# Small softmax turned by a transposing transfer, small steps spread over the engines, squares without a bias

## The chip, the cores and the metric

The kernel runs on one core of one Trainium2 chip. The metric is the device time of one execution in microseconds; of the kernel before three executions are known, and one more was taken with a profile. The core has TensorE (matrix products into PSUM), VectorE, ScalarE and GpSimd, which run side by side, each through its own list of instructions in order. SyncE (SP) issues all transfers here, also in order. In the profile the engines are PE, PEld (TensorE's weight loads), DVE, ACT, POOL and SPq.

## The reference

Four batches of 12608 tokens with 128 channels are computed in two parts. First agent attention with 49 agents a batch, and then a feed-forward layer of width 1024 whose activation is h times softmax(h), followed by a layer norm:

```python
a2k = sm(agents, k)            # softmax of the scaled products over 12608 keys
agent_v = a2k @ v              # 49 x 128 for each batch
q2a = sm(q, agents)            # "small softmax": 49 logits for each token
x = (q2a @ agent_v).reshape(B * S, 128)

h = x @ w_in                   # 128 -> 1024
e = np.exp(h - h.max(-1))
solu = h * e / (e.sum(-1) + 1e-9)
ln = (solu - mean(solu)) / sqrt(var(solu) + 1e-6) * g_ln
out = ln @ w_out               # 1024 -> 128
```

The factors 1/sqrt(128) and 1e-9 of the softmaxes are in the kernel; q, k and the agents are drawn eight times larger than unit inputs times 0.1.

## The kernel before

**Tiles.** A tile `x` is 128 tokens; there are 394, in four batches of 98 or 99. Two half tiles that are left at the ends of two batches share one tile (`both`). Units of 8 tiles (`UB`, 52 in all) go through the small softmax together.

**Phase A, once a batch** (`phase_a`). Keys and values come in 13 chunks of 512 KB each. For each chunk there are products with the agents (line 601), the chunk's maximum (`p1_max`, 606), the running maximum (`p1_nm`, line 613, VectorE), the exponential (627), four transposes, an eviction, and products with the values. At the end `agent_v` is multiplied into `w_in`, which gives 49 x 1024 matrices in two f16 halves. For batches 1 to 3 this is spread over the tiles of the batch before.

**Phase B, once a unit** (`phase_b`). Queries are loaded, logits made (863), maximum (869), subtraction (875), exponential (879), sum and reciprocal (883, 886). The result is packed as two f16 parts, high by ScalarE or GpSimd (`b4h`) and low by GpSimd (`b4l`, 897), into `packs`. Then TensorE turns the tiles four at a time into a PSUM bank (`b5`, line 904), and ScalarE or VectorE evicts the four to a buffer `pT` (`b6`, line 910), one of five (`PTB`).

**Steps of a tile.** H: four matmuls of `pT` with the matrices into one of two `ph` (955). Maximum and scaling on VectorE (983). Exponential on ScalarE (990). `u` = h times e on VectorE (998), with the sum of u accumulated into a cell `su`. The square on ScalarE (1019), with `su` as bias, sums the squared distances from the mean for the layer norm. Then u must be turned for the last product. For 331 tiles (`xbar`) GpSimd or ScalarE makes an f16 high half (`c_f0`, 1004 or 1006), GpSimd the low half (`c_f1`, 1009), and one transposing transfer of 128 x 2048 f16 on SP (`c_x`, line 1013) turns both into a buffer of the ring `xr` of eight (`XB`); 24 matmuls follow (1047). For the other 63 TensorE turns u in f32 (1026), ScalarE or VectorE evicts (1031) into a ring `tr` of eight (`TBUF`), and 16 passes follow. For each group of 8 or 16 tiles (27 groups) `c_rstd` makes the factor of the layer norm from the sums in a chain of short steps on GpSimd and ScalarE (1062 to 1085). VectorE multiplies four tiles of the product by it out of PSUM (`c_fin`, 1092), and a transfer writes eight tiles out (1098).

**Order.** The Python code makes a list of 6999 operations, each with the engines that may run it ("AD" is ScalarE or VectorE), its dependencies and a planned cost. A compressed table, `STEPS`, holds the order in which they are issued, and for those with two engines which one takes it. The instructions of each engine run in exactly this order:

```python
for i, k in todo:
    o = self.ops[i]
    e = o.eng[k]
```

The costs in the list serve only to choose a PSUM bank and to fill gaps in the head with idle matmuls. All transfers (queries, keys, values, outputs and the transposing ones) stand in one order on SP's queue; one that must wait holds up all behind it.

Of the kernel before, what the change touches and what calls it, by code (L numbers as in the profile page):

```python
# [49 lines left out]
    "sRmb16~5lK*jBq9dM72-f!&XNm#y1<daSwDvRa2H8jpuA+#~V+giYmX@TmF^IsriuSsytzP5MBkN1jmq!*9eRRi|WXXm~9Wct446J`T^%8dIjZ"  # L50
    "@O-s=nb7V8_5(d#715pJ;D@`Jee%?0=`bIV1NU{>9n<ngxVaHDR+(D668OwQN3W^hqv|v*Hzi%Tq8|XFszocG>vd~QZckjki)*_b8GUkSQlA`k"
    "x~ye}?n>YO==?+oIHLi3z_??`UK<VrRW7TqZ+KuIw@BwUW%fvSyzjC%(GVdj#%Ch?^Am1JK2Wx-7@cIVK4kSN%(J@rbe~7L;?vuS(Vg?5`OZbH"
    "tm0q(s?)599L?`))2&|H*6DDz5%(F+q>78W_=z{A0PBiV=?y+%ZYD+`L4b#&xT5!9_1NOqcfT8`Q|)%u5smK^yY^t}xLUJSf868lGsQIVu}%41"
    "Y^IkmDkf)b9W&>o0RXU1j+z6y@Hz=plxAVNS5GLY&ap1V=~i2;mr%5OZQ7BP&Cvs0eij*T-|hqFzx<2J)PQSc^Ss^t;m&IV>-8TEKz<kgn9@YX"
    "&VTHAqgDYo;QjWW{+*41{jS*$?`~?Ufg%=fnw`4r59(E*aZ0CXxDS|TO>Kj7wLKC0T>toYf8cGd3LO#V3IFzH|CGMBH)t~Zm(TV7z8OU_X4hA)"
    "Cgk1@m7-2LXR2SIROwbIQSgJF2KVgADcMO_jC;<5&UF~9$Eq@`Z;iC!D@V;RoZ|s!R(ExqsX9FggOfyZa^JA!)n7+Uk8hP-d#A}%b=P}!<=c^c"
    "Vy`=roINMAJ5^47Xd5T{0d5X#ruJ;$NH#HSy;YhjtKRujj)ebRrzv>k(?bU?xVBQZy@YBdcCt?lt&JTXlj+cI`uL~+O~;bc)-+lXQG?!{&5<p2"
    "`B7|YZ27k8v^pEnQ{Ec=w59g3@?l{_wY%+w$&(07zfII$wMDmjI;Q7B`)=9wk^#a_Y{NJ0j(Y#mPl2`8*1qkF<@nG3#8JE19=|3nM8G`bb+)R;"
    "l$4>(>Qftxq+dRAT<x6)<(}h5uWN~lw~Q|7H)pT?S9MF?wryo_YRm&#BTZ(AWNohC#!k{k)JF!L^7a(aUB<|OQ<3tR$Tn!&#+uGUG(|L*o5aLD"
    "0S1DXpza~uZ{7y+Xl2L(nFqIdw-h)vM~3W{?2dW8UHYA0IPUS>WZt{FTrx+;Qg^EBTyd(}+*=}3G1v8aXWJ6k4sRKZ&hYRuWen76TISv@2R%fr"  # L60
    "wx>hg^;3Tw^Sc1P-8ZV$<J9}i=(cHGJJo*FH7!?pJDNu=V83g>t(B4j&~l#cIRAwoy#lqCcxT$_uDb&x$(s4J6u(ubW34ya!SG#q*_urXbi~rH"
    "|G-AnfR8Te=|=UnBBCk3NvY1?x>tsm$m?>;apLWD$5B^B5+aX0SlRM%wBudMZLc14$;q;qW#r~64gtPi*{`;q9BFRx#N*uhj#>-GmHk(B_-*r5"
    "-Fo!Sf4THwV%ee|JCd&$8&=xV${EL)+CtVJ>0xqQx~v^IP@Wyi!7kyAoGYlY&=u+KO&M#!)yU4emL!MlBO9B(n#**Xb}<1o>A-xfKB`dPRLBF$"
    "$TaYGHXL?jsv-U~Rads&MnO;cVs%;9jC(Qbp*-zjhZMYT*sgXRc05)C?|J{m?V@vR!S$VQM;@oWbGpT)(b=gHGdPmo)BsP+|5zP^ve52}$@gND"
    "ZK<Bi2mzE=+uHKW9mn7JzY3RDT65U3;oc;O9aWdrxin*(N_8!0&$5If-~~Q;|H1hsX?uH^?MUEN;cA0J;e+~N&@qD#)Jab=y^UbcZB4#Y>~ycW"
    "&y>3ZgXG<!)3)PvT&(ZoaphUqpO|@Q^mdUxTcV3R2Veb4%B?pJf(nIuks3(Nc93_D8R)orvJ9%!rIfOBNqJSDD0|zpFzW88Y}o~msoI*Z%@(-V"
    "z-znMcFDnA)n423#h?BAAkhE2zg2goJG)Zfzn_b4w$-UC?;k1#-TuWB&D_c5;cC^_zL^}_)$C<cadNw5svpej{ZzWA3F4OW;<7FBc<YK%isOjF"
    "6>VGUsXrJ67XM%eK^|ue1B=-4a9r7_b~)Gev4i%#%jE8Qy~(E9b>UT{6ITq3?(1jQ<-hpDj)cqMTPH_1JC~Yl)2T6we=2c6q&Je|H;dBU3Hj=<"
    "<M8G_0poR0A6n~o$tSk)jt`2lo?7pXB{D^*cC?x)?TNNJSzCQb_Mfe!qU((ticZL<6Xlw|*T2)XAE(CNE$c%IY1JUGch{V3J0iekGggJEp0M8E"
    ")4nu%Rd>(_-k<y4gLhN6Mm%_n_e5OdgW;B5i@jmmeL$>iJ5@`yCm+XKZn|*LRiPVQSR;LDRi~|M`Pw<4+8ke42{mtlg@McZo|EiSOUMO)+)1Q0"  # L70
    "w<GJVu2g7!_GG{2s^OsisA(p%YS#@Mbdm=op}O_iJG{1o|MPX1bHx>`R5WzU#}!n2=fU6m?;Vb}^1ZCKu`zw<ik$DJhT1-uE*ds*16T@exwRc{"
# [95 lines left out]
class Plan:  # L167
# [8 lines left out]
    TRAIL = 0.2  # L176
# [59 lines left out]
def kernel(  # L236
# [26 lines left out]
    CPR = 1038.41  # L263
    PEP = (1, 8)
    PEN = 13
    XB = 8
    TBUF = 8
    FLEX = True
    UBUF = 6
# [1027 lines left out]
```

## Time and profile before

| What | Value |
|---|---|
| three executions | 1252.95, 1253.1 and 1257.48 us; median 1253.1 |
| the profiled execution's own time (span) | 1258.3 us |
| busy: TensorE, VectorE, ScalarE, GpSimd | 97, 95, 94, 89% |
| transposing transfers | 331 (2048 packets of 256 bytes each), four to six us from issue to landing in most pairs |
| loads and stores through SP | 105 MB |

The busy figures are shares of the whole span. Its first 40 us are the head, in which the first batch's keys and values are read and the weights prepared; the tail is the last 10 us. A figure such as 97% leaves open which engine holds the others up. For that the page is read stretch by stretch, with the chain that ended last and the list of waits. The DMA share is the mean over 16 engines of the time that their packets took; packets overlap in an engine, so it can pass 1.

### The profile page before, as it was taken

How to read it: one execution, taken by the hardware profiler on the slowest of the kernel's cores; microseconds unless marked ns; L12 is line 12 of the kernel's file. 1: busy time of each engine (PE TensorE's matmuls, PEld its weight loads, DVE VectorE, ACT ScalarE, POOL GpSimd, SP SyncE). 2: the span in 40 equal slices, each digit the busy share in tenths (PEclk: the TensorE clock that was granted, in tenths of full speed). 3: DMA queues.
4: the chain of work that ended last, by engine and by line, in shares of the span. 5: the costliest groups of instructions: out<-in, count | busy, mean ns of one | idle time of the engine just before them, and what ended most of it. 6: DMA issues, size and time to landing. Idle time of an engine off the chain costs nothing.

```text
span 1258.3 us, 36373 instructions
## 1 busy us (share of the span) xinstructions
PE 1214.6 (97%) x14304; PEld 936.6 (74%) x14304; DVE 1200.0 (95%) x2292; ACT 1183.8 (94%) x2212; POOL 1119.7 (89%) x889
## 2 busy tenths in 40 slices
PE   7989999999999999999999999999999999999998
PEld 4567777777777877777878777777787777777778
DVE  5799999999999999999999999899999999999997
ACT  5599999999999999999999999899999999999998
POOL 3488898999999898889999989789899999999995
PEclk8989999999999999999999999999999999999999
DMA  9599999999999999999999999999999899898896
GB/s 368 199 204 237 230 243 234 236 234 216 197 203 237 246 227 245 254 265 234 214 209 208 249 227 224 225 248 252 224 227 195 167 202 216 168 230 199 194 190 169
DMA packets 721516, 281.41 MB, mean 224 GB/s; under 512 B 692672, under 2 KB 696256, under 8 KB 721344
## 3 DMA queue, kind: packets, MB, share of 16 engines
q1 hardware_dynamic: 721344, 279.08, 103.2%
q8 instruction: 112, 1.84, 0.6%
q14 instruction: 60, 0.49, 0.1%
HBM read 79.67 MB, written 25.82 MB: 84 GB/s over the span
## 4 chain that ended last, share of the span: by engine, by line
ACT 24%; PE 24%; DVE 21%; issue 14%; POOL 9%; DMA 6%; SPq 0%; POOLq 0%; DVEq 0%; ACTq 0%
ACT ph L990 10%; PE px L1047 10%; PE ph L955 7%; ACT sq_b L1019 5%; ACT sq_a L1019 5%; DVE e_b L983 5%; DVE e_a L983 4%; PE px L654 2%; PE px L601 2%; DVE u_c L998 2%; DVE u_d L998 2%; DVE u_e L998 1%; DVE u_a L998 1%; PE px L1026 1%; DVE u_b L998 1%
## 5 line engine op out<-in xcount | busy, mean ns | idle before, releaser
L983 DVE TENSOR_SCALAR_CACHE_REDUCE e_a<-ph,nk 128x1024 f32<-128x1024 f32 x197 | 251.5, 1277 | 10.1 <-PE ph L955 9.2
L983 DVE TENSOR_SCALAR_CACHE_REDUCE e_b<-ph,nk 128x1024 f32<-128x1024 f32 x197 | 251.6, 1277 | 5.5 <-PE ph L955 5.0
L990 ACT ACTIVATE ph<-e_a,nm 128x1024 f32<-128x1024 f32 x197 | 219.3, 1113 | 16.3 <-DVE e_a L983 14.7
L990 ACT ACTIVATE ph<-e_b,nm 128x1024 f32<-128x1024 f32 x197 | 219.3, 1113 | 9.6 <-DVE e_b L983 8.4
L998 DVE SCALAR_TENSOR_TENSOR u_d<-e_b,cb,ph 128x1024 f32<-128x1024 f32 x66 | 84.2, 1276 | 2.2 <-ACT ph L990 1.9
L998 DVE SCALAR_TENSOR_TENSOR u_a<-e_a,cb,ph 128x1024 f32<-128x1024 f32 x66 | 84.1, 1275 | 1.8 <-ACT ph L990 1.4
L998 DVE SCALAR_TENSOR_TENSOR u_c<-e_a,cb,ph 128x1024 f32<-128x1024 f32 x65 | 82.8, 1274 | 2.3 <-ACT ph L990 1.3
L998 DVE SCALAR_TENSOR_TENSOR u_e<-e_a,cb,ph 128x1024 f32<-128x1024 f32 x65 | 82.8, 1274 | 1.6 <-ACT ph L990 1.1
L998 DVE SCALAR_TENSOR_TENSOR u_b<-e_b,cb,ph 128x1024 f32<-128x1024 f32 x65 | 82.9, 1276 | 1.2 <-ACT ph L990 0.6
L998 DVE SCALAR_TENSOR_TENSOR u_f<-e_b,cb,ph 128x1024 f32<-128x1024 f32 x65 | 82.7, 1273 | 1.3 <-ACT ph L990 0.7
L1047 PE MATMUL px<-wh,x_c 128*128 128x128 f16 x672 | 71.4, 220 | 2.6 <-DMA x_c<-f_e 2.3
L1047 PE MATMUL px<-wh,x_b 128*128 128x128 f16 x672 | 71.5, 219 | 1.1 <-DMA x_b<-f_a 0.7
L1047 PEld LDWEIGHTS <-x_b 128*128 128x128 f16 x1008 | 61.4, 98 | 14.8 <-issue 5.7
L1047 PEld LDWEIGHTS <-x_c 128*128 128x128 f16 x1008 | 62.4, 98 | 13.3 <-DMA x_c<-f_e 3.1
L1047 PE MATMUL px<-wh,x_a 128*128 128x128 f16 x672 | 70.1, 219 | 2.0 <-DMA x_a<-f_c 1.3
L1047 PEld LDWEIGHTS <-x_d 128*128 128x128 f16 x984 | 61.1, 99 | 14.3 <-issue 2.8
L1047 PEld LDWEIGHTS <-x_a 128*128 128x128 f16 x1008 | 61.7, 98 | 12.7 <-DMA x_a<-f_c 1.9
L1047 PE MATMUL px<-wh,x_d 128*128 128x128 f16 x656 | 69.5, 220 | 1.5 <-DVE u_c L998 0.7
L1047 PE MATMUL px<-wh,x_h 128*128 128x128 f16 x656 | 69.3, 219 | 1.7 <-DMA x_h<-f_c 1.3
L1047 PEld LDWEIGHTS <-x_h 128*128 128x128 f16 x984 | 60.5, 98 | 13.7 <-DMA x_h<-f_c 1.5
L1047 PEld LDWEIGHTS <-x_e 128*128 128x128 f16 x984 | 60.2, 98 | 13.2 <-issue 3.8
L1047 PE MATMUL px<-wh,x_g 128*128 128x128 f16 x656 | 68.5, 219 | 1.0 <-DMA x_g<-f_e 1.0
(457 smaller groups left out, 4733.3 us busy)
## 6 DMA issues: line engine op xcount, KB each, us to landing
qt_a<-in_qT_dram SPq DMA_DIRECT2D x24, 512.0 KB, 5.1
qt_b<-in_qT_dram SPq DMA_DIRECT2D x24, 512.0 KB, 5.2
out_dram<-ob_a SPq DMA_DIRECT2D x24, 512.0 KB, 3.7
out_dram<-ob_b SPq DMA_DIRECT2D x24, 512.0 KB, 3.6
kt_b<-in_kT_dram SPq DMA_DIRECT2D x18, 512.0 KB, 4.7
vt_b<-in_v_dram SPq DMA_DIRECT2D x18, 512.0 KB, 4.9
kt_a<-in_kT_dram SPq DMA_DIRECT2D x18, 512.0 KB, 5.0
vt_a<-in_v_dram SPq DMA_DIRECT2D x18, 512.0 KB, 4.8
```

What stands on the lines that cost most here:

```text
L601: nc.tensor.matmul(px[h * AP2 : (h + 1) * AP2, :w], ag_sb[:, b, :], kt[:, o : o + w], start=True, stop=True)
L654: nc.tensor.matmul(px[h * AP2 : (h + 1) * AP2, :C], eT[:w, o + h * AP2 : o + (h + 1) * AP2], vt[:w, t, :], start=all(z[0] != h for z in mm ...
L955: nc.tensor.matmul(ph[:, sl], w, m[:, sl], start=(q == 0), stop=(q == len(mm) - 1))
L983: nc.vector.tensor_scalar(out=nhs[x], in0=phs[x], scalar1=nks[k][:, j : j + 1], scalar2=None, op0=ALU.mult, op1=ALU.min, accum_out=nms[x])
L990: nc.scalar.activation(out=phs[x], in_=nhs[x], func=AF.Exp, scale=-1.0, bias=nms[x], accum_out=rs_[R]["S"][:, j : j + 1])
L998: nc.vector.scalar_tensor_tensor(out=u, in0=nhs[x], scalar=scal(x)[:, 4:5], in1=phs[x], op0=ALU.mult, op1=ALU.mult, accum_out=su)
L1019: nc.scalar.activation(out=sq, in_=u, func=AF.Square, bias=su, scale=-float(DF), accum_out=rs_[R]["Q"][:, j : j + 1])
L1026: nc.tensor.transpose(pt[:, kf * P : (kf + 1) * P], us[x][0][:, k0 * P : (k0 + 1) * P], ident)
L1047: nc.tensor.matmul(po, ut, wt[:, kf, :], start=(q == 0), stop=(q == len(mm) - 1))
```

## The change

- The small softmax is turned by one transposing transfer on SP for each unit of up to 8 tiles, from `packs` to a buffer of 128 x 8 x 128, one of three. The TensorE transposes, their PSUM banks and their evictions are gone; `b6` is left only for the two shared tiles.
- `p1_nm` and `c_nk` may run on GpSimd as well as VectorE, `c_fin` on ScalarE as well (then as one instruction for each tile).
- The square has no bias; it sums (sqrt(1024) u) squared. The sum of u goes to a table `U` of its group, and `r2` on GpSimd takes its square off: three more steps for each group.
- The ring for turned tiles has 13 buffers, five of them from the ring of the TensorE path, which keeps three.
- The order table is another one (6853 operations), and planned costs are changed.

```diff
@@ STEPS, the order table, is another one
...
@@ Plan.run, the planner's model of SP's queue (its numbers issue nothing; the order is read from the table)
...
-    TRAIL = 0.2
+    TRAIL = 0.15
+    TURN = 1.0
...
-                hold, pace, lag, turns = o.cost
-                self.at[e] = max(s + hold, self.dma - self.TRAIL) if turns else s + hold
-                o.end = self.dma = max(self.dma + pace, s + lag)
+                hold, pace, lag, sort = o.cost
+                a = s + 0.09 + hold
+                if sort == 1:
+                    a = max(a, self.dma - self.TRAIL)
+                elif sort == 0 and self.sort == 1:
+                    pace += self.TURN
...
@@ rings
-    XB = 8
-    TBUF = 8
+    XB = 13
+    TBUF = 3
+    HB = 8
...
-    PTB = 5
+    PTB = 3
...
-    LIFT = DF ** 1.5
+    LIFT = float(DF)
+    RN = DF ** 0.5
...
-    fr_, xr, tr = ring(FBUF, [P, 2, DF], F16, "f"), ring(XB, [P, 2 * NF, P], F16, "x"), ring(TBUF, [P, NF, P], F32, "t")
+    fr_, xr, tr = ring(FBUF, [P, 2, DF], F16, "f"), ring(HB, [P, 2 * NF, P], F16, "x"), ring(HB, [P, NF, P], F32, "t")
...
-    ekr, etr, ptr = ring(2, [P, HW], F32, "ek"), ring(2, [P, HW], F32, "eT"), ring(PTB, [P, GT * P], F16, "pT")
+    ekr, etr, ptr = ring(2, [P, HW], F32, "ek"), ring(2, [P, HW], F32, "eT"), ring(PTB, [P, UB, P], F16, "pT")
...
+    xs = xr + [t.bitcast(F16).rearrange("p k (z t) -> p (k z) t", z=2) for t in tr[TBUF:]]
...
@@ phase_a, running maximum
-            N1[c] = op("D", st(p1_nm, c), 0.13, at(z + (0.4 if head else ANM)), [E1[c], N1.get(c - 1)])
+            N1[c] = op("DG", st(p1_nm, c), (0.13, 0.4), at(z + (0.4 if head else ANM)), [E1[c], N1.get(c - 1)])
...
@@ phase_b
-        def b5(q, px):
-            m = min(GT, nt - q * GT)
-            px = r["pt", q] = px.bitcast(F16)
-            for j in range(m):
-                nc.tensor.transpose(px[:, j * P : (j + 1) * P], packs[k % 2][:, q * GT + j, :], ident16)
-
-        def b6(q, e):
-            m = min(GT, nt - q * GT)
-            pT = pTs[b, t0 // GT + q] = ptr[gidx[b, t0 // GT + q] % PTB]
-            px, cp = r.pop(("pt", q)), nc.scalar.copy if e == "A" else nc.vector.tensor_copy
-            cp(out=pT[:, : m * P], in_=px[:, : m * P])
-            if both(X0[b] + t0) and q == 0:
-                for i in range(2):
-                    cp(out=zp[:, i, i * AP2 : (i + 1) * AP2], in_=px[:, i * AP2 : (i + 1) * AP2])
+        def b5():
+            pTs[k] = ptr[k % PTB]
+            nc.sync.dma_start_transpose(out=pTs[k][:, :nt], in_=packs[k % 2][:, :nt].rearrange("p t c -> p (t c)"))
+
+        def b6(e):
+            for i in range(2):
+                o, z = zp[:, i, i * AP2 : (i + 1) * AP2], pTs[k][:, 0, i * AP2 : (i + 1) * AP2]
...
+        B5[k] = pT_op[k] = op("S", b5, (0.06 + 1.2 * nt / UB, 1.1, 2.2, 2), dues[5], [B4[k], last_hu.get(k - PTB)], shy=shy)
...
@@ the tile steps
-    def c_nk(k, x, m):
-        nk = nks[k] = tiny.tile([P, UB], F32, tag="nk", name=f"nk{k}")
+    def c_nk(k, x, m, e="D"):
+        nk = nks[k] = nkr[k % 4]
...
+            if e == "G":
+                nc.gpsimd.tensor_scalar(out=nk[:, j:i], in0=rsum[k][:, j:i], scalar1=c[:, 3:4], scalar2=None, op0=ALU.mult)
...
-                                       op0=ALU.mult, op1=ALU.mult, accum_out=su)
+                                       op0=ALU.mult, op1=ALU.mult, accum_out=rs_[R]["U"][:, j : j + 1])
...
-        pr[x] = xr[fl.index(x) % XB]
+        pr[x] = xs[fl.index(x) % XB]
...
-        nc.scalar.activation(out=sq, in_=u, func=AF.Square, bias=su, scale=-float(DF),
-                             accum_out=rs_[R]["Q"][:, j : j + 1])
+        nc.scalar.activation(out=sq, in_=us[x], func=AF.Square, scale=RN, accum_out=rs_[R]["Q"][:, j : j + 1])
...
         def r2():
+            gp.tensor_tensor(out=g("U"), in0=g("U"), in1=g("U"), op=ALU.mult)
+            gp.tensor_tensor(out=g("Q"), in0=g("Q"), in1=g("U"), op=ALU.subtract)
+            gp.tensor_scalar(out=g("Q"), in0=g("Q"), scalar1=0.0, scalar2=None, op0=ALU.max)
             gp.tensor_tensor(out=g("t"), in0=g("Q"), in1=g("t"), op=ALU.add)
...
-    def c_fin(G, j0, j1):
+    def c_fin(G, j0, j1, e="D"):
         ob = obr[G // 2 % 2][:, G % 2 * GT : (G % 2 + 1) * GT]
+        if e == "A":
+            R, r0 = rgrp[G * GT]
+            for j in range(j0, j1):
+                nc.scalar.mul(out=ob[:, j], in_=st[G]["po"][:, j * P : (j + 1) * P], mul=rs_[R]["yc"][:, r0 + j : r0 + j + 1])
+            return
...
```

## Rows read from the trace of the kernel before

**Rows 1.** Busy line of the page, section 1: busy us, share of the span, instructions.
```profile
PE 1214.6 (97%) x14304; PEld 936.6 (74%) x14304; DVE 1200.0 (95%) x2292; ACT 1183.8 (94%) x2212; POOL 1119.7 (89%) x889
```

**Rows 2.** Table of stretches: PE, PEld, DVE, ACT, POOL busy us (instructions), clock, DMA share, GB/s.
```profile
60.00:1200.00 1140.00, 1109.69 (x13201) 860.06 (x13201) 1110.84 (x2097) 1099.65 (x2044) 1053.18 (x812) 0.99 1.06 222
...
100.00:200.00 100.00, 98.49 (x1164) 74.39 (x1162) 97.51 (x187) 96.42 (x182) 86.93 (x67) 1.00 1.12 230
...
300.00:400.00 100.00, 96.51 (x1149) 74.41 (x1147) 97.29 (x185) 96.75 (x180) 95.80 (x76) 1.00 1.03 206
...
400.00:500.00 100.00, 100.00 (x1225) 79.21 (x1224) 98.89 (x184) 95.65 (x179) 92.34 (x71) 1.00 1.13 238
...
600.00:700.00 100.00, 98.57 (x1199) 77.35 (x1198) 98.59 (x191) 97.62 (x178) 95.44 (x74) 1.00 1.05 212
...
780.00:800.00 20.00, 17.02 (x177) 12.50 (x176) 15.04 (x27) 15.74 (x30) 14.45 (x10) 0.91 1.20 207
...
1000.00:1100.00 100.00, 96.38 (x1180) 76.28 (x1179) 99.21 (x180) 99.14 (x179) 98.01 (x75) 1.00 0.99 197
...
1100.00:1200.00 100.00, 93.33 (x1073) 72.59 (x1071) 98.70 (x176) 99.55 (x179) 97.56 (x73) 1.00 0.93 202
```

**Rows 3.** Chain that ended last: shares by engine (page); one piece: start us, us, what.
```profile
ACT 24%; PE 24%; DVE 21%; issue 14%; POOL 9%; DMA 6%; SPq 0%; POOLq 0%; DVEq 0%; ACTq 0%
...
778.46 9.73 DMA x_c<-f_e
```

**Rows 4.** Lines 910 (VectorE, then ScalarE) and 976 (VectorE) alone, whole span: busy us (instructions).
```profile
0.00:1258.00 1258.00, 8.34 (x20) 44.69 (x80) 0.99 1.04 224
...
0.00:1258.00 1258.00, 11.90 (x108) 0.99 1.04 224
```

**Rows 5.** TensorE: groups of line 904 (busy us, mean ns), then its timeline: start us, us.
```profile
L904 PE MATMUL px<-ident,pack 128*128 128x128 f16 x394 | 38.8, 221 | 1.1 <-POOL pack L897 1.1
...
601.27 0.39 PE L904 MATMUL px<-ident,pack 128*128 128x128 f16 x4
...
601.50 0.22 PE L1047 MATMUL px<-wh,x_h 128*128 128x128 f16 x1
```

**Rows 6.** Transposing transfers: SP's ns min/median/max of one pair; SP's timeline; landing us.
```profile
L1013 SPq DMA_TRANSPOSE x_a<-f_a x9: 1562/2176/3406, 63.9 to 1214.2; - x9
...
757.64 5.16 SPq L1013 DMA_TRANSPOSE x_f<-f_e  x1
...
789.79 1.87 SPq L1013 DMA_TRANSPOSE x_f<-f_c  x1
...
DMA to landing us min/median/max: 3.6/4.9/10.8
```

**Rows 7.** ScalarE and VectorE groups: busy us, mean ns of one, idle us before.
```profile
L1019 ACT ACTIVATE sq_a<-u_a,su_g 128x1024 bf16<-128x1024 f32 x17 | 19.4, 1140 | 0.0
...
L1004 ACT CAST f_d<-u_e 128x1024 f16<-128x1024 f32 x3 | 3.1, 1041 | 0.2 <-DVE u_e L998 0.2
...
L1071 ACT ACTIVATE y<-t 128x16 f32<-128x16 f32 x23 | 4.8, 207 | 1.2 <-POOL t L1067 1.1
...
L1073 ACT ACTIVATE y<-y,lnb 128x16 f32<-128x16 f32 x23 | 7.1, 308 | 0.7
...
L713 ACT COPY av_dup<-px x4: 243/246/265, 50.7 to 947.4; 128x128 f32<-128x128 f32 x4
...
L1092 DVE TENSOR_TENSOR ob_a<-px,yc 128x512 f32<-128x512 f32 x50 | 34.1, 684 | 1.2 <-POOL yc L1085 1.2
...
L613 DVE TENSOR_SCALAR nmp<-mxp,nmp 128x1 f32<-128x1 f32 x48 | 9.8, 205 | 0.3
```

**Rows 8.** GpSimd groups, the same columns.
```profile
L1006 POOL TENSOR_SCALAR f_e<-u_b 128x1024 f16<-128x1024 f32 x11 | 11.5, 1048 | 3.1 <-DMA x_a<-f_e 2.9
...
L1067 POOL TENSOR_TENSOR t<-Q,t 128x16 f32<-128x16 f32 x23 | 5.1, 221 | 5.5 <-ACT sq_b L1019 2.9 <-ACT sq_a L1019 1.8 <-ACT t L1062 0.6
...
L1082 POOL TENSOR_SCALAR z<-z,lif 128x16 f32<-128x16 f32 x23 | 8.1, 354 | 2.1
```

More of the change, by code (lines that the diff above doesn't have):

```diff
@@ L204, in run @@
             assert o.left == 0
-            s = max([self.at[e]] + [d.end + (self.LAT.get(d.by + e, 0.2) if d.by != "S" else 0.0) for d in o.deps])
+            s = max([self.at[e]] + [d.end + self.LAT.get(d.by + e, 0.2) for d in o.deps])
             if o.take:
@@ L214, in run @@
             if e == "S":
-                hold, pace, lag, turns = o.cost
-                self.at[e] = max(s + hold, self.dma - self.TRAIL) if turns else s + hold
-                o.end = self.dma = max(self.dma + pace, s + lag)
+                hold, pace, lag, sort = o.cost
[4 more added lines that the diff above has]
+                    pace += self.TURN
+                elif sort == 1 and self.sort == 0:
+                    lag += 0.3
+                self.at[e], self.sort = a, sort
+                o.end = self.dma = max(self.dma + pace, a + lag)
             else:
@@ L845, in qload @@
         return BQ[k]
-    groups, gidx = [], {}
     def phase_b(k, dues, gate=()):
@@ L930, in phase_b @@
         rsum["op", k] = op("D", b3r, 0.12, dues[3] + 0.2, [d3])
-        o4 = op("AG", b4h, (0.085 + 0.041 * nt, 0.08 + 0.051 * nt), dues[3] + 0.3, [a1] + [B5.get((k - 2, q)) for q in range(2)])
+        o4 = op("AG", b4h, (0.085 + 0.041 * nt, 0.08 + 0.051 * nt), dues[3] + 0.3, [a1, B5.get(k - 2)])
         B4[k] = op("G", lambda: b4l("G"), 0.16 + 0.088 * nt, dues[4], [o4])
-        for q in range(nq):
-            g = len(groups)
-            groups.append((b, t0 // GT + q))
-            gidx[groups[g]] = g
-            sc = min(GT, nt - q * GT) / GT
-            B5[k, q] = op("P", lambda px, q=q: b5(q, px), 0.02 + 0.21 * sc, dues[5] + 2.5 * q,
-                          [B4[k]] + (grp_h[groups[g - PTB]] if g >= PTB else []), take=True, shy=shy)
-            pT_op[groups[g]] = op("AD", lambda e, q=q: b6(q, e), (0.07 + 0.4 * sc + (0.4 if both(X0[b] + t0) and not q else 0), 0.13 + 0.27 * sc + (0.4 if both(X0[b] + t0) and not q else 0)), dues[5] + 2.5 * q + 0.3, [B5[k, q]], free=B5[k, q], shy=shy)
+        B5[k] = pT_op[k] = op("S", b5, (0.06 + 1.2 * nt / UB, 1.1, 2.2, 2), dues[5], [B4[k], last_hu.get(k - PTB)], shy=shy)
+        if both(X0[b] + t0):
+            pT_op[k] = op("AG", b6, (0.4, 0.5), dues[5] + 2.5, [B5[k]], shy=shy)
         if k + 2 < nu and k + 2 > 1:
@@ L988, in c_exp @@
         if R not in rs_:
-            rs_[R] = {z: tiny.tile([P, RT], F32, tag=z, name=f"{z}{R}") for z in "SQ"}
+            rs_[R] = {z: tiny.tile([P, RT], F32, tag=z, name=f"{z}{R}") for z in "SQU"}
         nc.scalar.activation(out=phs[x], in_=nhs[x], func=AF.Exp, scale=-1.0, bias=nms[x], accum_out=rs_[R]["S"][:, j : j + 1])
@@ L1025, in c_t @@
             k0 = hf * 4 + kf
-            nc.tensor.transpose(pt[:, kf * P : (kf + 1) * P], us[x][0][:, k0 * P : (k0 + 1) * P], ident)
+            nc.tensor.transpose(pt[:, kf * P : (kf + 1) * P], us[x][:, k0 * P : (k0 + 1) * P], ident)
     def c_ev(x, hf, k="A"):
```

323 lines of the change are left out of this document (158 added, 165 removed).

## The prediction

> **What bounds the kernel now.** First the busy line of the page [rows 1]: TensorE 1214.6, VectorE 1200.0, ScalarE 1183.8 and GpSimd 1119.7 us of 1258.3. Four engines stand between 89 and 97%, so no share names the bound; the stretches must. In the table of stretches [rows 2] the middle (60 to 1200) leaves VectorE 1140 - 1110.8 = 29 us idle, TensorE 30, ScalarE 40, GpSimd 87. There is little slack to squeeze; time can fall almost only where work falls. The late stretch 1000:1100, with no keys and values left to load, has GpSimd at 98.0, VectorE and ScalarE at 99.2 and 99.1: there GpSimd binds as much as the others. The stretch 780:800 is the opposite: VectorE is busy for 15.0 of 20 us, and the chain [rows 3] holds a transposing transfer of 9.73 us just there. The share of that chain by engine is ACT 24, PE 24, DVE 21, issue 14, POOL 9, DMA 6%: the bound passes round, and a gain on one engine alone would be passed on to the next.
>
> The sum is made against the profiled 1258.3 us. That execution is 5.2 us above the median of the runs (1253.1) and close to their slowest (1257.48), so I carry differences over to 1253.1.
>
> **The change part by part.** Which engine takes an operation that may run on two stands in the order table. Read entry by entry against the operations in the order in which the code makes them, it gives the counts below.
>
> *Small softmax turned by transfer.* 394 transposes on TensorE and 100 evictions go. The evictions are 20 on VectorE, 8.3 us, and 80 on ScalarE, 44.7 us [rows 4]. On TensorE they are 38.8 us in all (394 of about 221 ns that overlap); but a group of four begins at 601.27 and the next matmul at 601.50 [rows 5], so a group displaces 0.23 us, 23 us for the 100. TensorE gains 23 to 39; I take 31, the middle. 52 transposing transfers come onto SP's queue, most of half the size of the 331 that are there.
>
> *Price of a small transfer.* A large one holds SP for 1.56 us at least, 2.18 in the median of one tile pair [rows 6]. Half the bytes bound a small one at 0.78 from below, the whole price at 2.18 from above; I take half the median, 1.09, as the row 789.79 (1.87 us) lies nearer to a price by bytes than the 5.16 of row 757.64, which follows three loads. 52 x 1.09 = 57 us of queue. What hides it: the DMA share is 1.12 to 1.13 in the stretches with loads and 1.20 in 780:800, where the engines did wait for a transfer [rows 2]. That leaves about 6 us in 100; 52 x 100 / 1258 = 4.1 small ones cost 4.5. It fits, barely. Against it stands what the table gives back: plain transfers come in 69 runs between transposing ones, before in 109, and the wait of 5.16 us behind three loads shows that a turn costs. Without that cover it is the first rival. Queued behind a small transfer that waits for GpSimd's second half of the pack are all large ones, and TensorE's last matmuls wait for those. 47 of the 52 are issued 8 to 17 tiles ahead of use, so they can land 4.9 us after issue [rows 6] and none is late; the others are a rival.
>
> The Trainium skill speaks against this step: "VectorE: DVE Perf Modes", section "The three transpose paths", gives 390 ns on TensorE and 1309 ns by DMA for a square of 128 x 128, and advises TensorE where PSUM will do as destination. By it 394 squares would be 516 us of transfers, an estimate. The trace does not agree for squares that travel together: 16 in 1.56 to 2.18 us [rows 6] are 0.10 to 0.14 us each.
>
> *Square without bias.* 394 squares read a bias pointer and take 1140 ns. The nearest operation of that shape without one is the cast, 1041; and of the two small activations the one with a bias takes 308, the one without 207 [rows 7]. Both say 0.10 us; bounds 0 and 0.14 (the rows are other functions). 394 x 0.10 = 39 us off ScalarE. GpSimd pays in the 27 groups: three more steps, two tensor-tensor at 0.221 and one with immediates, between 0.221 and 0.354 [rows 8], so 0.74 x 27 = 20 us.
>
> *Small steps off VectorE.* 17 of 52 of line 613 go to GpSimd: 17 x 0.205 = 3.5 us less. 33 of 52 of line 976: 11.9 x 33 / 52 = 7.6 less [rows 4, 7]. 20 of 100 output scalings of line 1092 go to ScalarE: 20 x 0.684 = 13.7 less [rows 7]. On GpSimd the 50 small steps cost 0.22 to 0.354 each [rows 8]; at the upper price 17.7 us. On ScalarE a scaling becomes four instructions; the copy of 128 x 128 is 246 ns without a pointer [rows 7], with one about 0.1 more, so 0.25 to 0.35 each; at 0.30, 20 x 4 x 0.30 = 24 us.
>
> *Shifted by the order.* The high half f0 goes to ScalarE 68 times, before 33: 35 x 1.041 = 36.4 us more there, 35 x 1.048 = 36.7 less on GpSimd [rows 7, 8]. Five evictions more go to VectorE, five fewer to ScalarE: 5 x 0.684, the row of a scaling of that shape, is 3.4 us more, 5 x 44.7 / 80 = 2.8 less [rows 4, 7].
>
> *Rings.* Thirteen buffers for turned tiles (five of them from the TensorE path, which keeps three), and three units of softmax. Issue to SP comes a tile later after u than before (3.3 tiles for 2.3) and the last matmuls 2.4 tiles after it (3.1 before); I cost it at nothing as long as the transfers keep their pace, and else in the first rival.
>
> **The sum.** VectorE: -8.3 - 13.7 - 3.5 - 7.6 + 3.4 = -29.7. ScalarE: -44.7 - 39.4 + 36.4 + 24 - 2.8 = -26.5. GpSimd: -36.7 + 17.7 + 20 = +1. TensorE -31. Three ways to make one time of it: were VectorE the bound all through, -29.7; if the three vector engines share the work evenly, (-29.7 - 26.5 + 1) / 3 = -18.4; weighted by the chain [rows 3], 0.24 x 26.5 / 1183.8 + 0.24 x 31 / 1214.6 + 0.21 x 29.7 / 1200 = 1.67%, -21.0. I take -22, near the last two, since the bound passes round, and a little towards the first: profile 1236, median 1253.1 - 22 = 1231. Once the VectorE steps are gone, GpSimd is what is late next, as it loses no work.
>
> **The rivals.**
> A. *The transfers become the bound* (slower). If a small transfer costs as much as a large one, 2.18 us, the loaded stretches need 4.1 x 2.18 = 9 us in 100 where 6 are free; it decides from 6 / 4.1 = 1.45 us each. Six such stretches are loaded (two in each of three batches): 18 us, and one stall of 5 us as at 780:800 in each of the three loading batches, 15. Outside, about half of the gain, 11, remains: 1253 + 33 - 11 = 1275. For it: share 1.13 of 1.20, the 9.73 us. Against it: fewer turns, a deeper ring, and that DMA has only 6% of the chain. The Trainium skill's 1309 ns above points the same way.
> B. *GpSimd holds the end.* Where it is at 95% and more (95.8, 95.4, 98.0 and 97.6 in the four such stretches of [rows 2], 400 us) nothing is gained: -22 x 860 / 1258 = -15, 1238. For it: its sum of +1. Against: in the last stretch more f0 go to ScalarE.
> C. *Late units.* Three of the last six small transfers are issued one or two tiles (about 3.2 us each) ahead of use; with 4.9 us to land each stalls up to 3 us: +9, 1240.
> D. *The square gets no shorter.* ScalarE then ends at +13 beside VectorE's -30: the even share is (-29.7 + 12.9 + 1) / 3 = -5, 1248, no change that can be told. Against: both pairs in [rows 7].
>
> **How the numbers follow.** Forecast 0.52 (1231, own range 1222 to 1238), A 0.14, B 0.20, C 0.08, D 0.06. No change means within 0.5%, 6.3 us, about what a measurement of this kernel can tell. Forecast, B and C are faster by more than that, 0.80; I move 0.05 of it to no change and slower together, since a part of the sum may be lost to a wait that none of these names: faster 0.75, same 0.10, slower 0.15. The range takes the forecast, B, C and D with the upper ends of the unknown prices, and the full -30 and TensorE's -39 below: 1214 to 1256.
>
> **What would show it.** VectorE near 1170, ScalarE near 1157, GpSimd near 1121, TensorE 1176 to 1192 us busy. The square near 1041 ns; the scalings on ScalarE 0.25 to 0.35 us. SP holds a small transfer for about 1.1 us. Waits of TensorE for turned tiles stay a few us long in sum. The prediction fails if small transfers hold SP for more than 1.45 us and waits for turned tiles head the list (A), or if VectorE's idle time in the middle grows well past 29 us.

## The result, and the profile after it

The changed kernel takes 1262.99 us in the median (1258.02 to 1268.01, 12 runs) where the kernel before takes 1253.03 (1250.67 to 1257.48, 12 runs): ratio 1.0072, interval 1.0054 to 1.0091. It is slower by 0.7%, outside the forecast range, and on the other side of it.

The two profiled spans lie closer (1258.3 before, 1256.2 after), since the one of before was taken in an execution near the slow end of its runs and the one of after near the fast end: the ratio says how much, and the profiles say where.

The busy line of the page after, which answers to [rows 1]:

```profile
PE 1192.8 (95%) x13912; PEld 916.6 (73%) x13912; DVE 1178.7 (94%) x2172; ACT 1165.0 (93%) x2242; POOL 1116.5 (89%) x986
```

The work did fall: TensorE by 21.8 us, VectorE by 21.3, ScalarE by 18.8, GpSimd by 3.2. None of it arrives in the time. The stretches after show why, in the columns of [rows 2]:

```profile
60.00:1200.00 1140.00, 1090.22 (x12847) 842.16 (x12846) 1090.94 (x1981) 1084.20 (x2078) 1050.96 (x904) 0.99 1.12 234
...
100.00:200.00 100.00, 92.82 (x1085) 70.68 (x1082) 89.37 (x162) 89.48 (x176) 84.85 (x76) 0.98 1.16 232
...
880.00:900.00 20.00, 15.32 (x163) 12.02 (x162) 12.73 (x24) 14.04 (x30) 15.25 (x15) 0.83 1.18 256
...
1000.00:1100.00 100.00, 95.68 (x1164) 75.17 (x1162) 99.50 (x173) 99.38 (x186) 97.19 (x80) 1.00 1.09 221
```

VectorE idles 1140 - 1090.9 = 49 us in the middle, where it idled 29. The late stretch 1000:1100, without key and value loads, is as full as before (99.5); 100:200 fell from 97.5 to 89.4. The idle time sits where loads run, and in holes: 880:900 is a second 780:800 [rows 2], with VectorE busy for 12.7 of 20 us. In the chain, ScalarE, TensorE and VectorE gave way to GpSimd and to DMA, which went from 6 to 14%:

```profile
POOL 20%; PE 18%; issue 16%; ACT 14%; DMA 14%; DVE 12%; SPq 0%; POOLq 0%; DVEq 0%; ACTq 0%
```

Waits, 60 to 1200 us (us in total, times, longest), some of each list, first before, then after:

```profile
DVE e_a L983 <- PE ph L955: 9.2, 11, 3.7
DVE e_b L983 <- PE ph L955: 5.0, 9, 1.6
```

```profile
DVE e_a L973 <- PE ph L942: 19.3, 19, 5.5
DVE e_b L973 <- PE ph L942: 15.6, 17, 4.4
...
POOL f_e L996 <- DMA t_g<-f_e: 5.8, 1, 5.8
...
PEld L1035 <- DMA x_a<-f_b: 4.1, 1, 4.1
PEld L1035 <- DMA t_g<-f_e: 4.0, 1, 4.0
```

Read from the bottom: TensorE waits for a turned tile in its last matmuls, so the next `ph` is late, so VectorE waits for `ph` (34.9 us in these two rows, 14.2 before). All waits of TensorE's weight loads for turned tiles, summed over the buffers, are 34.1 us, before 14.7. GpSimd waits for the same transfers, since they free the buffers that it fills. One such hole on SP's timeline (start us, us):

```profile
872.66 1.93 SPq L1003 DMA_TRANSPOSE t_g<-f_e  x1
874.68 3.17 SPq L1003 DMA_TRANSPOSE t_h<-f_a  x1
877.94 1.26 SPq L898 DMA_TRANSPOSE pT_a<-pack  x1
879.25 0.57 SPq L840 DMA_DIRECT2D qt_a<-in_qT_dram  x1
879.88 0.44 SPq L840 DMA_DIRECT2D qt_b<-in_qT_dram  x1
880.42 0.38 SPq L582 DMA_DIRECT2D kt_b<-in_kT_dram  x1
880.84 0.43 SPq L588 DMA_DIRECT2D vt_b<-in_v_dram  x1
881.31 0.44 SPq L588 DMA_DIRECT2D vt_a<-in_v_dram  x1
881.85 6.90 SPq L1003 DMA_TRANSPOSE x_a<-f_b  x1
```

SP is never free here. GpSimd's second half of `f_b` (start us, us) ends at 874.69:

```profile
872.55 2.14 POOL L999 TENSOR_TENSOR f_b<-u_e,f_b 128x1024 f16<-128x1024 f32 x1
```

Its transfer begins at 881.85, behind a large one, a small one (1.26) and five loads, and then holds SP for 6.90 us, as it follows the loads: in this trace a large one holds SP for 2.0 us in the median behind another transposing one and for 6.7 behind five plain ones. Two neighbouring pieces of the chain are:

```profile
881.81 0.04 POOL f_d L999
881.85 10.48 DMA x_a<-f_b
```

The chain goes back from the transfer to GpSimd's `f_d`, which this transfer does not need. That is a limit of the view: it puts the start of a transposing transfer down to what GpSimd was at just then. If the chain is followed along SP's own order instead (from a transfer to its tile only where that tile was finished after SP's previous instruction), SP's queue has 36% of it after, 11% before, and 17% in the run without small transfers below; GpSimd has 11, 9 and 13%.

**A measure that the prediction lacked.** Two sums over SP's timeline say what the DMA share does not. First, for how long of 100 us SP is held by transfers (small ones, large ones and loads together); second, how long on average a filled tile waits for SP, from the end of GpSimd's second half to the start of its transfer (mean of the tiles in the stretch, us). "No small" is the second experiment.

```
stretch from          100  200  300  400  500  600  700  800  900 1000 1100
SP held, before        88   92   78   90   87   76   91   90   71   75   66
SP held, after         96   90   86   96   95   94   93   96   81   83   75
SP held, no small      92   80   82   93   95   82   91   86   69   74   64
tile waits, before    2.4  2.7  1.0  1.4  2.0  0.6  3.2  2.0  0.8  1.0  0.6
tile waits, after     4.4  3.4  1.6  2.7  5.7  1.9  2.7  5.3  1.0  0.9  0.7
tile waits, no small  2.7  1.4  1.1  2.3  4.6  1.0  2.1  2.5  0.5  0.2  0.2
```

In the six loaded stretches (100, 200, 400, 500, 700 and 800) SP was held for 87 to 92 us of 100 before, and after for 90 to 96. Without the small transfers it is 80 to 95, although 100 us of that faster run hold more tiles. Over all 331 tiles the wait for SP went from 1.48 to 2.54 us; without the small transfers it is 1.61.

### The profile page after: what moved, and what is told of

It reads as the page before. It is cut to its first block, busy times and chain, and to the rows that moved or that the text cites. A ratio compares the mean times of both kernels' runs of the same rounds, so it can differ in the third digit from the quotient of the medians.

```text
span 1256.2 us, 35751 instructions
## 1 busy us (share of the span) xinstructions
PE 1192.8 (95%) x13912; PEld 916.6 (73%) x13912; DVE 1178.7 (94%) x2172; ACT 1165.0 (93%) x2242; POOL 1116.5 (89%) x986
## 4 chain that ended last, share of the span: by engine, by line
POOL 20%; PE 18%; issue 16%; ACT 14%; DMA 14%; DVE 12%; SPq 0%; POOLq 0%; DVEq 0%; ACTq 0%
PE px L1035 9%; ACT ph L980 6%; PE ph L942 5%; ACT sq_b L1008 3%; DVE e_b L973 3%; POOL f_d L999 3%; POOL f_e L999 2%; ACT sq_a L1008 2%; DVE e_a L973 2%; POOL f_b L999 2%; POOL f_a L999 2%; POOL f_c L999 2%; POOL f_b L996 1%; POOL f_e L996 1%; POOL f_a L996 1%
## 5 line engine op out<-in xcount | busy, mean ns | idle before, releaser
L942 PE MATMUL ph<-mh,pT_a 128*128 128x512 f16 x264 | 100.5, 381 | 9.6 <-DVE u_a L988 2.6
L942 PE MATMUL ph<-mh,pT_b 128*128 128x512 f16 x260 | 98.9, 380 | 4.7 <-DVE u_a L988 1.9
L942 PE MATMUL ph<-mh,pT_c 128*128 128x512 f16 x260 | 99.3, 382 | 3.9 <-DVE u_c L988 1.7
L942 PE MATMUL ph<-ml,pT_a 128*128 128x512 f16 x264 | 100.5, 381 | 0.0
L942 PE MATMUL ph<-ml,pT_c 128*128 128x512 f16 x260 | 99.0, 381 | 0.0
L942 PE MATMUL ph<-ml,pT_b 128*128 128x512 f16 x260 | 98.7, 380 | 0.0
L988 DVE SCALAR_TENSOR_TENSOR u_c<-e_a,cb,ph 128x1024 f32<-128x1024 f32 x65 | 82.9, 1275 | 2.8 <-ACT ph L980 1.2
L988 DVE SCALAR_TENSOR_TENSOR u_d<-e_b,cb,ph 128x1024 f32<-128x1024 f32 x66 | 84.2, 1275 | 0.7 <-ACT ph L980 0.3
L988 DVE SCALAR_TENSOR_TENSOR u_f<-e_b,cb,ph 128x1024 f32<-128x1024 f32 x65 | 82.9, 1275 | 1.6 <-ACT ph L980 1.5
L973 DVE TENSOR_SCALAR_CACHE_REDUCE e_a<-ph,nk_d 128x1024 f32<-128x1024 f32 x49 | 62.6, 1277 | 9.4 <-PE ph L942 8.9
L1008 ACT ACTIVATE sq_a<-u_a 128x1024 bf16<-128x1024 f32 x66 | 69.5, 1053 | 0.7 <-DVE u_a L988 0.2
L1008 ACT ACTIVATE sq_a<-u_c 128x1024 bf16<-128x1024 f32 x66 | 69.3, 1050 | 0.8 <-DVE u_c L988 0.5
L1008 ACT ACTIVATE sq_b<-u_f 128x1024 bf16<-128x1024 f32 x65 | 68.4, 1052 | 1.5 <-DVE u_f L988 1.0
```

The costliest lines, as they stand in the source:

```text
L942: nc.tensor.matmul(ph[:, sl], w, m[:, sl], start=(q == 0), stop=(q == len(mm) - 1))
L973: nc.vector.tensor_scalar(out=nhs[x], in0=phs[x], scalar1=nks[k][:, j : j + 1], scalar2=None, op0=ALU.mult, op1=ALU.min, accum_out=nms[x])
L988: nc.vector.scalar_tensor_tensor(out=u, in0=nhs[x], scalar=scal(x)[:, 4:5], in1=phs[x], op0=ALU.mult, op1=ALU.mult, accum_out=rs_[R]["U"][ ...
L1008: nc.scalar.activation(out=sq, in_=us[x], func=AF.Square, scale=RN, accum_out=rs_[R]["Q"][:, j : j + 1])
```

## The experiments

A ratio is always to the kernel before, run on the same chip together with it. The diffs are shortened. Three questions: is it the small transfers; is it their number or their bytes; and is it them alone.

**Shorter runs of plain transfers** (63 moves of 54 of them, so that few stand more than two in a row):

```diff
         todo = steps()
+        for i, j in MOVES:      # 63 pairs: plain transfer i behind transposing transfer j
+            e = next(e for e in todo if e[0] == i)
+            todo.remove(e)
+            todo.insert(next(n for n, z in enumerate(todo) if z[0] == j) + 1, e)
```

> The changed kernel with 63 of SP's plain transfers put behind a later transposing one, so that plain runs are 1 or 2 long and not up to 7; nothing else moves. Theory 1 (a transposing transfer behind a long plain run lands late and stalls TensorE, 8.9 us of hold at 162.68): the waits on turned tiles shrink, about 1250 us, 1% below the changed kernel's 1263. Theory 2 (the queue has too much to move; each turn between plain and transposing costs it 1.5 us more): 69 runs become about 105, so 1270 or more. Theory 3 (the order of the compute engines is at fault, not the transfers): 1263.

Measured: 1282.32 us, ratio 1.0214 (1.0189 to 1.0240). This is theory 2: 37 more turns between plain and transposing transfers cost 18 us, some 0.5 each, although few runs are long. Large transfers hold SP for 904 us, after 866, and the weight loads' waits for turned tiles grow from 34 to 55 us in sum, while waits for keys and values grow by some 2 us. The order's grouping of loads is a gain and not the cause.

**No small transfers** (all but the first three left out; later units reuse what those turned):

```diff
-            nc.sync.dma_start_transpose(out=pTs[k][:, :nt], ...
+            if k < PTB:
+                nc.sync.dma_start_transpose(out=pTs[k][:, :nt], ...
```

> The changed kernel without 49 of its 52 small transposing transfers: the first three units' turned softmax is used again for all later units, so that part of the computation is left out. Theory 2: 49 x 1.3 = 64 us go from SP's queue, the time falls to 1240 or below. Theory 1: the long plain runs remain, 1258. Theory 3: 1263.

Measured: 1229.9 us (1228.11 to 1233.71), ratio 0.9802 (0.9777 to 0.9827). Busy line and chain:

```profile
PE 1184.0 (97%) x13912; PEld 911.3 (74%) x13912; DVE 1178.1 (96%) x2172; ACT 1162.9 (95%) x2242; POOL 1114.9 (91%) x986
```

```profile
PE 32%; ACT 16%; DVE 15%; issue 13%; POOL 9%; DMA 8%; DVEq 0%; SPq 0%; ACTq 0%; POOLq 0%
```

VectorE, ScalarE and GpSimd do the same work as in the changed kernel within some 2 us. The 49 transfers left out are worth 1.0072 - 0.9802 = 2.7%, 34 us or 0.7 us each; without them the kernel takes 0.9802 of the time before, 1228 us where the forecast had 1231. In the changed kernel the small ones hold SP for 76 us in all (from 60 us on), and the large ones for 866, where they hold it for 842 without the small ones. What the run also takes away is any wait for a small transfer to land. In the changed kernel only one engine waits for one, GpSimd (us, times):

```profile
  POOL pack L889: 1.4, 2
```

So the 34 us are not paid by units that come late, but by what shares the queue with them.

**The old order with small transfers:**

```diff
-        def b5(q, px):        # 4 transposes on TensorE
-        def b6(q, e):         # eviction
+        def b5(q, px):        # at the place of the first group of a unit
+            pTs[k] = ptr[k % HB]
+            nc.sync.dma_start_transpose(out=pTs[k][:, :nt], in_=packs[k % 2][:, :nt]...)
+        def b6(q, e):         # names the slice only
```

> The kernel before, in its own order, with one thing changed: the small softmax is turned by one transposing transfer for each unit, issued where the first of its TensorE transposes stood; 394 TensorE transposes and 100 evictions go. Theory 2: 68 us of queue on top of the old 109 turns, 1270 or more. Theory 1: plain runs are short here, and TensorE and ScalarE lose 23 and 45 us of work, 1245. Theory 3: 1245 as well.

Measured: 1297.5 us, ratio 1.0349 (1.0314 to 1.0384). In an order that was not made for them the same 52 transfers cost more, though TensorE and ScalarE lose 10 and 28 us of work. Chain:

```profile
DVE 23%; POOL 18%; issue 17%; DMA 14%; ACT 14%; PE 12%; SPq 1%; POOLq 0%; DVEq 0%; ACTq 0%
```

**The old order with the square without bias:**

```diff
-    LIFT = DF ** 1.5
+    LIFT = float(DF); RN = DF ** 0.5
-        nc.scalar.activation(out=sq, in_=u, func=AF.Square, bias=su, scale=-float(DF), ...
+        nc.scalar.activation(out=sq, in_=u, func=AF.Square, scale=RN, ...
         def r2():
+            ...   # three GpSimd steps on "U" and "Q"
```

> The kernel before, in its own order, with the square without bias and the three more GpSimd steps for each of 27 groups; nothing else. If ScalarE's work counts at its share of the chain (24%), 39 us less give 0.24 x 39 / 1184 = 0.8%, and GpSimd's 20 us more take 0.2% back: 1245. If the fixed order passes the time on to another engine: 1253.

Measured: 1260.68 us, ratio 1.0036 (1.0019 to 1.0053). Busy line and chain:

```profile
PE 1212.2 (96%) x14304; PEld 935.5 (74%) x14304; DVE 1200.3 (95%) x2292; ACT 1159.5 (92%) x2212; POOL 1136.5 (90%) x970
```

```profile
POOL 26%; PE 20%; DVE 19%; issue 17%; DMA 10%; ACT 7%; SPq 0%; POOLq 0%; DVEq 0%; ACTq 0%
```

ScalarE loses 24.3 us, GpSimd gains 16.8, and the chain moves to GpSimd.

**The same without the three steps** (kernel before, square only):

```diff
         def r2():
-            ...   # three GpSimd steps on "U" and "Q"
```

> The kernel before with the square without bias but without the three GpSimd steps that correct for the mean (their part of the variance is left out, so its output is another). Theory that those steps took the gain back (they put 17 us on GpSimd, and the chain went to GpSimd for 26 us in 100): 1244 to 1249, ratio 0.993 to 0.996. Rival (in this order ScalarE's 24 us lie beside other work, and a shorter square only waits longer): within 0.3 per cent of before, ratio 0.998 to 1.002, with GpSimd steps costing the 0.36 per cent measured with them.

Measured: 1253.27 us, ratio 0.9965 (0.9948 to 0.9982). So in the old order the square is worth 0.35% and the three steps cost 0.7%. With them GpSimd has 26% of the chain, without them 9%: it held the end there.

**The changed kernel without the three steps:** the same edit on the changed kernel.

> The changed kernel without the three GpSimd steps for each 16 tiles that correct the square for the mean (that part of the variance is left out, so the output is another). In the old order they cost 0.36 - (-0.35) = 0.7 per cent. If GpSimd holds the end in the changed order too (20 us in 100 of its chain), the ratio falls from 1.0072 to about 1.000 to 1.003. If the x transfers hold it, within 0.2 per cent of the changed kernel, 1.005 to 1.009. I say 1.006.

Measured: 1262.24 us, ratio 1.0059 (1.0038 to 1.0081); the interval contains the changed kernel's 1.0072. GpSimd has 20% of the page's chain after the change, but taking 18 us of its work away (1098.6 us busy) changes nothing that can be told: much of that share is SP's, as shown above.

**Half of each small transfer:**

```diff
-            nc.sync.dma_start_transpose(out=pTs[k][:, :nt], in_=packs[k % 2][:, :nt]...
+            m = nt if k < PTB else nt // 2
+            nc.sync.dma_start_transpose(out=pTs[k][:, :m], in_=packs[k % 2][:, :m]...
```

> The changed kernel, each small transfer from the fourth unit on turning only the first half of its unit's tiles (the other half of the buffer keeps what an earlier unit left there, so the output is another); count, order and waits stay. If the price goes by what the transfer holds of SP and of the engines, by size: half of the 33 us goes, 1246, ratio 0.994. If it goes by count (one more turn between plain and transposing transfers, one more entry of the queue): 1262, ratio 1.007. I say 1248: the hold should fall from 1.3 to about 0.8 us.

**One tile of each small transfer:** the same with `1` in the place of `nt // 2`.

> The changed kernel, each small transfer from the fourth unit on turning one tile of its unit instead of eight (32 KB instead of 256; the other seven keep what an earlier unit left, so the output is another). Half the size took the ratio from 1.0072 to 0.9964, where no small transfers at all gave 0.9802. If the price is a part for each transfer and a part by size, these three give 0.0054 for the count and 0.0216 for the size, and an eighth of the size 0.9802 + 0.0054 + 0.0027 = 0.988. If the price is mostly that a transposing transfer holds SP, whose hold hardly fell (1.31 to 1.26 us), 0.995 to 1.000. I say 0.990.

Measured: 1252.31 us, ratio 0.9964 (0.9946 to 0.9983) for half, 1244.25, ratio 0.9925 (0.9903 to 0.9948) for one tile. The first row is of the changed kernel, the second with half, the third with one tile (ns min/median/max that SP is held, then first and last start):

```profile
L898 SPq DMA_TRANSPOSE pT_a<-pack x18: 1232/1310/2502, 39.7 to 1228.2; - x18
```

```profile
L898 SPq DMA_TRANSPOSE pT_a<-pack x18: 1217/1259/2213, 39.9 to 1227.8; - x18
```

```profile
L898 SPq DMA_TRANSPOSE pT_a<-pack x18: 1168/1225/2072, 40.6 to 1213.4; - x18
```

The hold hardly depends on the size: 1.31, 1.26 and 1.23 us for 256, 128 and 32 KB; I expected 0.8 for half. The time does. Above the ratio without small transfers lie 0.0270, 0.0162 and 0.0123 for full, half and an eighth: a straight line through them has about 0.009 that no size takes away and 0.017 that goes by bytes. So some 12 us of the 34 are paid by the number of transfers, 0.25 us each, and some 22 by their bytes. In SP's timeline the bytes show in the large transfers: they hold SP for 866, 859 and 844 us from 60 us on, and for 842 with no small ones. Why they do, in SP's issue or in the DMA engines, no run shows. My 0.990 for one tile, from the first three points, gave too little to the number; the reading by the hold alone gave too much. With these intervals the split is good to about a quarter of the whole. It rests on the medians: the one profiled execution with half (1257.5 us) is as long as that of the changed kernel (1258.0).

**TensorE again in the new order.** 51 units by transposes and evictions, each put a step behind the place of the transfer; then only the 31 units near loads:

```diff
+        def t5(q, px):            # 4 transposes into a PSUM bank
+        def t6(q, e):             # eviction, ScalarE and VectorE in turn
...
+        for c, i, k in self.more[::-1]:
+            todo.insert(c, (i, k))     # at place c of the order
```

> The changed kernel with its order, but the small softmax of 51 of the 52 units is turned by TensorE again: 98 groups of transposes and 98 evictions, alternating between ScalarE and VectorE, put into the order a step behind the place where the small transfer stood (one unit, for which no PSUM bank is free there, keeps its transfer). All else of the change stays: square without bias, small steps on GpSimd and ScalarE, the order of the late tiles. Theory of SP's queue: the 33 us that the small transfers cost go away as they did in the run without them (1229.9), and what comes is engine work, 49 evictions of 0.40 us on VectorE and 49 of 0.47 us on ScalarE and 98 x 0.21 us on TensorE, some 20 us on each engine: between 1232 (all of it in waits) and 1250 (all of it on the path), I say 1243, ratio to before 0.99. Rival theory (the order of the change was made for transfers and is bad with anything else): 1262 or more, ratio 1.007 or more.

> As the run before, but only the 31 units whose small transfer stands within five SP entries of a key or value load go back to TensorE; 21 units, in stretches in which SP was held 64 to 83 us in 100, keep the transfer. Theory of SP's queue: a small transfer costs where the queue is full and next to nothing where it has room, so 1230 plus at most 31/51 of the engine work of the run before: 1232 to 1244, I say 1238, ratio 0.985, and faster than the run with 51 units. Rival: each transfer costs its 0.65 us wherever it stands, a price of the turn and not of a full queue: 1230 + 21 x 0.65 + 11 = 1255, ratio 1.00, and slower than the run with 51 units.

Measured: 1345.88 us, ratio 1.0711 (1.0677 to 1.0745), and 1295.52, ratio 1.0307 (1.0275 to 1.0340). The first lies where the rival had it (over 1262), the second where neither theory had it; the places were bad. TensorE's weight loads wait at these transposes, in the run with 51 units (us, times, longest):

```profile
PEld L954 <- issue: 56.2, 39, 5.4
```

In the kernel before, only 0.6 us are lost ahead of them in this way, and 3.0 to the pack. By the planner's own count of the banks, three or all four of the four are taken at 31 of the 52 places where a small transfer stands. These two runs say nothing on the transfers' price.

**The same, placed where a bank is free,** for 51 units and for 30 (the edit is a list of other places).

> As the run in which 51 units are turned by TensorE, where TensorE stood idle before these transposes for over 50 us, for PSUM banks above all; now each group of transposes and its eviction stands at a place of the order where a bank is free and the engines have room. Theory of SP's queue: without the small transfers the kernel takes 1230; 98 groups of four transposes are 37 us on TensorE, 49 evictions of 0.42 us are 21 us on VectorE, 49 of 0.565 us are 28 us on ScalarE; TensorE had 42 us idle in the run without transfers, so half of the 37 is on the path: 1248, ratio 0.993, between 1232 and 1267. Rival (the change's order bears nothing but transfers, wherever the transposes stand): over 1275, as in that run.

> As the run before, for the 30 units that stand near key and value loads; 22 units keep their transfer, most of them in stretches in which SP was held 64 to 83 us in 100. Theory of SP's queue, where a transfer costs only where the queue is full: 1230 plus 30/51 of the 18 us of the run before and a few us for the transfers: 1243, ratio 0.988. Rival, a price of 0.65 us for each transfer wherever it stands: 1230 + 11 + 14 = 1255, ratio 0.998. Rival, the order bears nothing but transfers: over 1270.

Measured: 1274.87 us, ratio 1.0157 (1.0131 to 1.0183), and 1258.49, ratio 1.0027 (1.0009 to 1.0045). Both are slower than the theory of SP's queue had them: the first stands at the bound of the rival by which the order bears nothing but transfers (1275), the second nearest to the rival with one price wherever a transfer stands (0.998). The waits at the transposes have gone from 56 to 11 us; one other is new, in the run with 51 units (us, times, longest): GpSimd cannot write the next pack while transposes that come too late still read the old one.

```profile
POOL pack L931 <- PE px L954: 34.2, 8, 8.1
PEld L954 <- issue: 11.0, 12, 4.3
```

So the transfers are dear, but this order has no cheap place for the transposes either: in it 51 units on TensorE cost more than 51 transfers. The mixture is the better one. Where the time goes shows tile by tile: the start of `u` (line 988) of a tile, in us behind the same tile in the run without small transfers.

```
tile                    16   48   96  112  208  224  256  272  304  384
changed kernel        -0.6  6.2  7.2 11.6 16.2 20.3 23.0 29.6 29.7 29.7
30 units by TensorE    1.1  4.6 17.7 18.2 20.7 22.6 26.1 28.1 28.5 30.3
18 units by TensorE   -0.6  5.9  6.5 10.9 16.1 18.8 21.6 24.1 23.9 23.9
```

The changed kernel loses its 30 us in a few stretches, and nothing after tile 272, where a small transfer every 8 tiles goes on: there SP has room and the price is zero. That speaks against one price wherever a transfer stands.

**TensorE where the tiles are late:** the 18 units 16 to 24 and 28 to 36; then the 11 units 16, 17 and 28 to 36.

> The changed kernel; only the 18 units 16 to 24 and 28 to 36 are turned by TensorE, at the places of the run with 30 such units, the other 34 by transfers. Tile by tile the changed kernel falls 30 us behind the run without small transfers, and it does so in a few places: 6 us before tile 48, 22 us between tiles 96 and 272, nothing after; the run with 30 units by TensorE lost only 10 us between tiles 96 and 272 but 18 before. Theory that the transfer costs where x transfers are late and nothing elsewhere: 7 us up to tile 96 as in the changed kernel, 10 after it: 1230 + 17 = 1247, ratio 0.993, faster than both kernels. Rival, a price for each transfer wherever it stands: 34 x 0.65 + 8 = 30, 1260, ratio 1.004.

> As the run before with TensorE for the 11 units 16, 17 and 28 to 36 alone, those whose transfers stand where the changed kernel falls behind most (around 350 to 410 and 690 to 905 us). Theory that the transfer costs where x transfers are late: 7 us up to tile 96, 5 between tiles 112 and 208 as in the changed kernel, 8 at the places changed: 1230 + 20 = 1250, ratio 0.995. Rival, a price for each transfer: 41 x 0.65 + 5 = 32, 1262, ratio 1.006.

Measured: 1252.63 us (1247.98 to 1257.76), ratio 0.9968 (0.9950 to 0.9985), and 1255.77, ratio 1.0005 (0.9986 to 1.0025). Both fall between the theories. The first is faster than both kernels, by 0.3% and by 1.0%, with this busy line:

```profile
PE 1196.4 (96%) x14056; PEld 922.1 (74%) x14056; DVE 1186.2 (95%) x2194; ACT 1170.4 (94%) x2256; POOL 1116.5 (89%) x986
```

It does 3.6 to 7.5 us more work than the changed kernel on TensorE, VectorE and ScalarE, and is 1% faster: the mean wait of a tile for SP is 1.78 us, after 2.54. It loses as expected up to tile 96 (6.5) but 17.6 instead of 10 between 96 and 272.

## Why the prediction was wrong

*The step that failed* is the cover of the small transfers: "It fits, barely". It took the DMA share as the measure of room, 1.13 where it was busy and 1.20 where the engines waited, and read 6 us in 100 from it. The height of that share beside a wait is no capacity: after the change it is 1.16 in 100:200, below the 1.20, and VectorE is down to 89.4 there. SP's own timeline had the answer before the run: 87 to 92 us of 100 held in the loaded stretches. 4.1 small transfers at 1.31 are 5.4 us more in 100, and the large ones hold SP longer with them too. The 52 transfers were costed at nothing, and the 49 that could be left out cost 34 us; that is more than the gain of 22, and 1253 - 22 + 34 = 1265 is what was measured (1263).

*Price of a small transfer.* 1.09 us was forecast; 1.31 was measured in the median, but 1.5 in the mean (76 us for the 51 from 60 us on), as the few behind loads hold SP for up to 4.4. The prediction's sum needs the mean, and that is past the 1.45 from which rival A was to decide. The point itself came from the same headroom and fell with it. The scaling by bytes behind 1.09 is wrong too: the hold is near 1.25 us down to 32 KB.

*Rival A* is the mechanism that came true, at 1263 instead of 1275: transfers as the bound in the loaded stretches, stalls behind loads. Its reason, that a small transfer costs as much as a large one, did not come true; its signs did: waits for turned tiles more than doubled (34.1 us for 14.7, which was more than "a few us" already before, though the list's single rows are headed by others), and VectorE idles well past 29 us (49). It had a chance of 0.14, for the sake of DMA's 6% in the chain; a share in the chain says what a resource costs now, not how near it is to its limit, and along SP's own order SP had 11% beside it. The turns given back were right in sign (the first experiment), and too small to pay for this.

*The engine work.* VectorE -21.3 (forecast -29.7), ScalarE -18.8 (-26.5), TensorE -21.8 (-31, with 23 as the lower end), GpSimd -3.2 (+1). TensorE's lower end, the displaced time of a group [rows 5], was the right one. On ScalarE the square did as forecast: its record fell by 0.09 us (forecast 0.10), and the next instruction begins 0.95 us behind its start, where it began 1.04 behind, 36 us in all. The evictions were sized too large: their 44.7 us are records by themselves, which begin before the record ahead of them ends, and only 37.8 lie outside it. A scaling on ScalarE takes 0.36 us instead of 0.30. After, in the columns of [rows 7]:

```profile
L1008 ACT ACTIVATE sq_a<-u_c 128x1024 bf16<-128x1024 f32 x66 | 69.3, 1050 | 0.8 <-DVE u_c L988 0.5
...
L1086 ACT ACTIVATE ob_b<-px,yc 128x128 f32<-128x128 f32 x48 | 13.5, 361 | 0.0
```

*The sum over the engines* held nonetheless: work some 20 us less on three engines gave 0.9802 of the time before where the transfers were out of the way, 1228 us against 1231. That the two agree so closely is partly luck, as the terms for these three engines were a third too large and TensorE did 8.8 us less still in that run.

The advice of the Trainium skill that the prediction set aside ("VectorE: DVE Perf Modes", section "Rules for kernel authors": TensorE where PSUM will do) was not right for its figure, since eight squares cost 0.7 us here and not 8 x 1.3; but taking 18 units back to TensorE did pay.

*Rival B* (GpSimd) holds in the old order, where the three steps cost 0.7%, and not in the new one. *Rival C* (late units) is not seen: after tile 272 nothing is lost, and TensorE waits for no small transfer. *Rival D* is out: the square takes 1.05 us instead of 1.14.

## What to carry to other kernels

Before work goes to a queue, add up how long that queue is held in each stretch, and how long filled buffers wait for it; a busy share of the DMA engines beside a wait is no limit, and a resource with 6% of the chain can be at its limit. Where the chain passes through a queue, see whether the step that it names is the one that the transfer needed, or whether the queue was held. A transfer added to a full queue is paid by what stands behind it: the small ones cost nothing where SP was held for 83 us of 100 or less, and some 0.9 us each (30 us for the 34 that were left out up to tile 272) in the stretches before, where it was held for 86 to 96. When engine work falls and the time does not, compare the start of one instruction per tile with a run that leaves the suspect out: the loss shows in a few places, and only those need mending.

## What the runs showed of the hardware that I had not expected

A transposing transfer of 32 to 256 KB holds SP for 1.23 to 1.31 us in the median, almost whatever its size, and 256 KB land a median 3.6 us after issue. Moving plain transfers so that they alternate more with transposing ones cost 1.4%. A square on ScalarE that loses its bias pointer is 0.09 us shorter. GpSimd can stand first in the page's chain (20%) and 18 us of its work be worth nothing.
